# Handing tile 3's normalization to ScalarE and tile 1's to VectorE, and splitting a power on GpSimd, in the prologue of a transformer block

## The chip, the cores and the metric

The kernel runs on one core of a Trainium2 chip. The metric is device time in microseconds of one launch; the lower the better. In the profile the engines are PE (TensorE, matmuls), PEld (its weight loads), DVE (VectorE), ACT (ScalarE), POOL (GpSimd) and SP (SyncE); L1596 is line 1596 of the kernel. The profile also records the clock that TensorE was granted, 1.000 being full speed.

## The reference, cut to what matters

One transformer block over a sequence of 2048 rows of 512 columns: layer norm, a modulation by `1 + ca` and `sa` that come from a small vector `c` through `silu` and a matrix, attention with 32 heads over a window of 512 cached keys, a residual, a second modulated layer norm and a dense layer with relu.

```
def _layernorm(x, axis=-1, eps=1e-05):
    m = jnp.mean(x, axis=axis, keepdims=True)
    v = jnp.var(x, axis=axis, keepdims=True)
    return (x - m) / jnp.sqrt(v + eps)
...
mod = (_silu(c) @ w_mod).reshape(c.shape[0], 6, 1, -1)
...
h = _layernorm(x, axis=-1) * (1 + ca) + sa
x = x + ga * _A_ref(h, A_k_cache, A_v_cache, A_wq, A_wo)
```

The change concerns only the first of these layer norms, and of it only the first block of 512 rows: four tiles of 128 rows x 512 columns. The first projection and the scores of this block wait for them.

## The kernel before: the parts that the change touches

Every instruction goes to one engine's stream, in program order, with the semaphores that its inputs need. `warm(n)` issues n dummy matmuls of 512 columns whose results nobody reads. The statistics of tiles 0, 1, 2 are VectorE's (`ln_stat`), those of tile 3 are ScalarE's (a sum, then a sum of squares into `s3`).

```
    # rstd = (var + eps) ** -0.5, the power on GpSimd, hi - lo columns
    def rstd_pow(lo, hi):
        kb.op(POOL, lambda e: e.tensor_tensor(rstd[:, lo:hi], rstd[:, lo:hi], cst[:, 0:1].to_broadcast([P, hi - lo]), op=ALU.pow), ...)
    ...
    ln_stat(0)
    warm(3, [R_mv[0]])          # dummies, after the statistics of tile 0
    ln_stat(1)
    warm(2, [R_mv[1]])
    rstd_add(0, 2)
    rstd_pow(0, 2)
    kb.op(POOL, ...)            # bias for tile 1: -mean * rstd
    kb.op(ACT, ...)             # ScalarE normalizes tile 1
    silu_mul()
    ln_stat(2)
    rstd_add(2, 3)
    rstd_pow(2, 4)              # tiles 2 and 3 in one instruction
    ln_norm(0)                  # VectorE normalizes tile 0
    kb.op(POOL, ...)            # GpSimd normalizes tile 3
    ...
    fs = mod_cols_mm(0, QBK)    # 32 one-column matmuls on four pieces of w_mod
    for f in fs:
        f()
    ln_tposes(0, TB[0])
    mod_cols_evac(0, QBK)       # VectorE: the modulation vectors, called modc
    ...
    ln_tposes(1, TB[0])
    warm(2, bk=6)
    ln_norm(2)                  # VectorE normalizes tile 2
    mod_half(0, 0, DVE); mod_half(0, 2, ACT)     # modulation of tiles 0 and 1
    ln_tposes(2, TB[1]); ln_tposes(3, TB[1])
    mod_half(0, 1, DVE); mod_half(0, 3, ACT)
    q_half(0, 0, CC_ORDER, QBK)                  # first projection, first half
    mod_half(1, 0, DVE); mod_half(1, 2, ACT); mod_half(1, 1, DVE); mod_half(1, 3, DVE)
    ...                                          # second half, then the scores
```

## Time and profile before

| | us |
|---|---|
| time, median of the first three runs | 560.69 (560.68 to 560.93) |
| span in the profile | 558.9 |
| VectorE's first normalization (tile 0) starts; ScalarE's of tile 1 starts at 7.74 | 7.94 |
| first score matmul starts | 12.41 |

The page and the chain that ended last are read in the prediction below. One more view: TensorE alone in the first 14 us of the kernel before. Columns: start in us, duration in us, engine, line, operation, output and inputs, shapes, count; in brackets the idle time and who ended it.

```profile
8.40 0.62 PE L1377 MATMUL psS<-ident,xn 128*128 128x128 bf16 x8
...
9.42 0.34 PE L1377 MATMUL psS<-ident,xn 128*128 128x128 bf16 x3
...
9.97 0.34 PE L1377 MATMUL psS<-ident,xn 128*128 128x128 bf16 x3 [0.16 <-POOL xn L1613]
...
12.41 0.59 PE L1374 MATMUL psS<-qT,kT 128*128 128x512 bf16 x2 [0.17 <-DVE qT L1620]
```

The transposes of tiles 0 and 1 run together from 8.40, those of tile 2 start at 9.42, those of tile 3 only at 9.97, when GpSimd has finished. The last line is the first score matmul. From there TensorE is busy to the end (98% of the span in the page; 13.89 us of the 14 from 14 to 28 us), so its start is the figure to watch.

### The profile page before, as it was taken

Reading aid. Unit: us, or ns where it says so; the run is one execution under the profiler, and the core shown is the slowest. Engines: PE = TensorE matmul, PEld = TensorE weight load, DVE = VectorE, ACT = ScalarE, POOL = GpSimd, SP = SyncE. Lnnn points to the kernel's source line nnn. Section 1 sums busy time; section 2 is a strip of 40 time slices with the busy share of each in tenths; the row PEclk is TensorE's granted clock in tenths of the full one; section 3 lists DMA queues with packets and bytes.
Section 4 is the critical chain, followed back from the end, with each engine's and each line's share of the span. In section 5 each row is a group of like instructions: output and inputs, shape, how many; then the busy total and the mean of one; then the engine's idle time right before and its main releaser. Section 6 shows DMA issues by size and latency. Waiting matters only on the chain.

```text
span 558.9 us, 9675 instructions
## 1 busy us (share of the span) xinstructions
PE 549.5 (98%) x4061; PEld 315.5 (56%) x4135; DVE 254.7 (46%) x555; ACT 349.3 (63%) x453; POOL 53.3 (10%) x50
## 2 busy tenths in 40 slices
PE   8999999999999999999999999999999999999997
PEld 4665555555555555555555555555555554444444
DVE  4455555553546544335445443333354438322134
ACT  5986666666666666666666666666666644432500
POOL 2000022004410000033000000332000000000000
PEclk9999999999999999999999999999999999999999
DMA  9999662522225144353352412121214110200001
GB/s 258 257 203 192 137 162 47 114 43 73 39 41 74 39 84 106 62 129 58 95 95 56 76 40 39 39 38 38 39 39 76 39 29 0 49 28 22 21 29 48
DMA packets 113357, 42.66 MB, mean 76 GB/s; under 512 B 93977, under 2 KB 112153, under 8 KB 113305
## 3 DMA queue, kind: packets, MB, share of 16 engines
q1 hardware_dynamic: 112584, 41.08, 35.5%
q10 hardware_dynamic: 720, 0.89, 0.5%
q8 instruction: 33, 0.54, 0.4%
q14 instruction: 20, 0.16, 0.1%
HBM read 18.35 MB, written 2.10 MB: 37 GB/s over the span
## 4 chain that ended last, share of the span: by engine, by line
PE 97%; issue 1%; DVE 1%; DMA 1%; POOL 0%
PE psS L1374 28%; PE psO L1374 27%; PE psQ L1374 23%; PE psW L1374 19%; DMA x<-in_A_x_dram 1%; DVE st L1384 0%; POOL xn L1613 0%; POOL rstd L1596 0%; DVE mv L1385 0%; DVE qT L1620 0%; PE psS L1377 0%; DVE rstd L1593 0%; DVE PT L1734 0%; DVE PT L1736 0%; DVE tmp L1424 0%
## 5 line engine op out<-in xcount | busy, mean ns | idle before, releaser
L1498 ACT ACTIVATE PT<-psS 128x1024 bf16<-128x1024 f32 x256 | 262.7, 1028 | 128.7 <-PE psS L1374 128.5
L1374 PE MATMUL psS<-qT,kT 128*128 128x512 bf16 x510 | 151.4, 379 | 0.3 <-DVE qT L1620 0.2
L1374 PEld LDWEIGHTS psO<-v,PT 128*128 128x128 bf16 x2048 | 126.6, 98 | 30.2
L1374 PE MATMUL psO<-v,PT 128*128 128x129 bf16 x2048 | 137.0, 220 | 0.0
L1374 PE MATMUL psQ<-hT,wq 128*128 128x512 bf16 (+1 forms) x509 | 130.2, 377 | 0.2
L1508 DVE RECIPROCAL rinv<-psO 128x4 f32<-128x4 f32 x128 | 23.3, 182 | 225.6 <-PE psO L1374 225.6
L1374 PE MATMUL psW<-wo,oT 128*128 128x512 bf16 x452 | 118.1, 379 | 3.1
L1509 DVE TENSOR_TENSOR o<-psO,rinv 128x512 bf16<-128x512 f32 x128 | 88.5, 691 | 4.5
L1374 PEld LDWEIGHTS psQ<-hT,wq 128*128 128x128 bf16 x512 | 49.9, 98 | 59.8 <-DVE qT L1488 0.4
L1374 PEld LDWEIGHTS psS<-qT,kT 128*128 128x128 bf16 x512 | 49.6, 98 | 58.8 <-ACT PT L1498 0.5
L1490 ACT ACTIVATE qT<-psQ 128x512 bf16<-128x512 f32 x125 | 74.1, 593 | 0.0
L1723 ACT ACTIVATE wq<-psS 128x512 bf16<-128x512 f32 x56 | 33.4, 597 | 49.1 <-PE psS L1374 49.1
L1374 PEld LDWEIGHTS psW<-wo,oT 128*128 128x128 bf16 x512 | 44.9, 98 | 32.9 <-DVE acc L1531 1.2
L1531 DVE TENSOR_TENSOR acc<-psW,acc 128x512 f32<-128x512 f32 x48 | 33.2, 691 | 6.7 <-PE psW L1374 6.7
L1374 PE MATMUL psO<-wmw,wq 128*128 128x512 bf16 (+1 forms) x165 | 32.8, 352 | 0.2
L1534 POOL TENSOR_TENSOR acc<-acc,gaf 128x512 f32<-128x512 f32 x12 | 15.6, 1301 | 146.8 <-DVE acc L1531 139.8
L1390 POOL TENSOR_TENSOR rstd<-rstd,cst 128x4 f32<-128x4 f32 x7 | 7.2, 1025 | 215.7 <-DVE rstd L1389 215.7
L1734 DVE TENSOR_TENSOR PT<-psO,gbf 128x512 f32<-128x512 f32 (+1 forms) x12 | 7.5, 624 | 40.4 <-PE psO L1374 40.4
L1374 PE MATMUL psS<-h2T,wmw 128*128 128x512 bf16 x110 | 25.2, 379 | 0.1
L1374 PEld LDWEIGHTS psO<-wmw,wq 128*128 128x128 bf16 x168 | 15.3, 98 | 16.6
L1374 PE MATMUL psS<-hT,wmw 128*128 128x512 bf16 x110 | 24.4, 379 | 0.1
L1384 DVE BATCH_NORM_STATS2 st<-x 128x6 f32<-128x512 bf16 x31 | 21.1, 680 | 3.6 <-DMA x<-in_A_x_dram 3.6
(90 smaller groups left out, 192.0 us busy)
## 6 DMA issues: line engine op xcount, KB each, us to landing
wo<-in_A_wo_dram SPq DMA_DIRECT2D x4, 1024.0 KB, 6.5
wq<-in_A_wq_dram SPq DMA_DIRECT2D x7, 512.0 KB, 4.6
wmw<-in_B_w_dram SPq DMA_DIRECT2D x14, 256.0 KB, 3.1
wmw<-in_w_mod_dram SPq DMA_DIRECT2D x4, 512.0 KB, 5.1
oT<-o SPq DMA_TRANSPOSE x128, 2.4
out_dram<-PT SPq DMA_DIRECT2D x15, 128.0 KB, 1.7
x<-in_A_x_dram SPq DMA_DIRECT2D x3, 512.0 KB, 4.4
v<-in_A_v_cache_dram SPq DMA_DIRECT2D x8, 128.0 KB, 4.1
```

The costliest lines, as they stand in the source:

```text
L1374: kb.op(PE, lambda e: e.matmul(out_ap, lhsT, rhs, start=start, stop=stop), reads=reads, group_writes=[R_b[k] for k in bk], signal=signal)
L1384: kb.op(DVE, lambda e: e.bn_stats(st[:, t, :], x_sb[:, t, :]), reads=[R_x[t]], writes=[R_st[t]])
L1390: kb.op(POOL, lambda e: e.tensor_tensor(rstd[:, sl], rstd[:, sl], cst[:, 0:1].to_broadcast([P, hi - lo]), op=ALU.pow), reads=R_rstd[sl] + ...
L1490: kb.op(ACT, lambda e: e.activation(qT[u % NQT][:, :], bank[bk], ACTF.Copy), reads=[R_b[bk]], writes=[R_qT[u % NQT]])
L1498: kb.op(ACT, lambda e: e.activation(PT[u % NPT][:, pr * 2:pr * 2 + 2, :], s_ps[pr][:, :, :], ACTF.Exp, scale=scale), reads=[R_b[pr * 2], R ...
L1508: kb.op(DVE, lambda e: e.reciprocal(rinv[:, u, :], o_ps[:, :, P]), reads=[R_b[5], R_b[6]], writes=[R_rinv])
L1509: kb.op(DVE, lambda e: e.tensor_tensor(o_sb[u % NOS][:, :, :], o_ps[:, :, 0:P], rinv[:, u, :].unsqueeze(2).to_broadcast([P, TPB, P]), op=A ...
L1531: kb.op(DVE, lambda e: e.tensor_tensor(acc[:, tl, :], bank[WBK], acc[:, tl, :], op=ALU.add), reads=[R_b[WBK], R_acc[tl]], writes=[R_acc[tl]])
L1534: kb.op(eng, lambda e: e.tensor_tensor(acc[:, tl, :], acc[:, tl, :], gaf[:, :], op=ALU.mult), reads=[R_acc[tl], R_ga], writes=[R_acc[tl]])
L1723: kb.op(ACT, lambda e: e.activation(h1T[b % 2][:, fc, :], bank[bk], ACTF.Relu), reads=[R_b[bk]], writes=[R_h1[b % 2][fc]], pre=all_events( ...
L1734: kb.op(DVE, lambda e: e.tensor_tensor(yt[i][:, c0:c1], bank[bk][:, c0:c1], gbf[:, c0:c1], op=ALU.mult), reads=[R_b[bk], R_gb], writes=[R_ ...
```

## The change

Its intent: let tile 3 not wait for GpSimd's 512-column normalization. ScalarE, which took that tile's statistics, normalizes it; VectorE takes tile 1, which ScalarE had; GpSimd raises tile 3's variance to its power on its own, earlier, and tile 2's afterwards.

```
     rstd_pow(0, 2)
-    kb.op(POOL, lambda e: e.tensor_scalar(s3[:, 3:4], mv[:, 1, 0:1], rstd[:, 1:2], -1.0, op0=ALU.mult, op1=ALU.mult), ...)
-    kb.op(ACT, lambda e: e.activation(xn[:, 1, :], x_sb[:, 1, :], ACTF.Identity, bias=s3[:, 3:4], scale=rstd[:, 1:2]), ...)
+    rstd_pow(3, 4)
+    kb.op(POOL, lambda e: e.tensor_tensor(s3[:, 3:4], s3[:, 1:2], rstd[:, t3:t3 + 1], op=ALU.mult), ...)
+    kb.op(ACT, lambda e: e.activation(xn[:, t3, :], x_sb[:, t3, :], ACTF.Identity, bias=s3[:, 3:4], scale=rstd[:, t3:t3 + 1]), ...)
     silu_mul()
     ln_stat(2)
     rstd_add(2, 3)
-    rstd_pow(2, 4)
+    rstd_pow(2, 3)
     ln_norm(0)
-    kb.op(POOL, lambda e: e.tensor_scalar(xn[:, t3, :], x_sb[:, t3, :], s3[:, 1:2], rstd[:, t3:t3 + 1], op0=ALU.add, op1=ALU.mult), ...)
+    ln_norm(1)
```

(The lists of reads and writes are cut; t3 is 3.)

More of the change, by code (lines that the diff above doesn't have):

```diff
@@ L1604, in build_fast @@
     rstd_pow(0, 2)
-    kb.op(POOL, lambda e: e.tensor_scalar(s3[:, 3:4], mv[:, 1, 0:1], rstd[:, 1:2], -1.0, op0=ALU.mult, op1=ALU.mult), reads=[R_mv[1], R_rstd[1]], writes=[R_nmr])
-    kb.op(ACT, lambda e: e.activation(xn[:, 1, :], x_sb[:, 1, :], ACTF.Identity, bias=s3[:, 3:4], scale=rstd[:, 1:2]),
-          reads=[R_x[1], R_nmr, R_rstd[1]], writes=[R_xn[1]])
+    rstd_pow(3, 4)
+    kb.op(POOL, lambda e: e.tensor_tensor(s3[:, 3:4], s3[:, 1:2], rstd[:, t3:t3 + 1], op=ALU.mult), reads=[R_s3, R_rstd[t3]], writes=[R_nmr])
+    kb.op(ACT, lambda e: e.activation(xn[:, t3, :], x_sb[:, t3, :], ACTF.Identity, bias=s3[:, 3:4], scale=rstd[:, t3:t3 + 1]),
+          reads=[R_x[t3], R_nmr, R_rstd[t3]], writes=[R_xn[t3]])
     silu_mul()
@@ L1610, in build_fast @@
     rstd_add(2, 3)
-    rstd_pow(2, 4)
+    rstd_pow(2, 3)
     ln_norm(0)
-    kb.op(POOL, lambda e: e.tensor_scalar(xn[:, t3, :], x_sb[:, t3, :], s3[:, 1:2], rstd[:, t3:t3 + 1], op0=ALU.add, op1=ALU.mult),
-          reads=[R_x[t3], R_rstd[t3], R_s3], writes=[R_xn[t3]])
+    ln_norm(1)
     TB = [[0, 0, 2, 2], [1, 1, 3, 7]]
```

## The prediction

> **What bounds the kernel now.** I read the page's shares first, then its chain of work that ended last, then the order of instructions in the first 14 us, then the list of who waited for whom there. The page's first two parts:
>
> ```profile
> PE 549.5 (98%) x4061; PEld 315.5 (56%) x4135; DVE 254.7 (46%) x555; ACT 349.3 (63%) x453; POOL 53.3 (10%) x50
> ...
> PE   8999999999999999999999999999999999999997
> ```
>
> TensorE is busy for 98% of the 558.9 us span; only the first slice (14 us) and the last are below 9 tenths. The edited lines run once each, all before 10 us, so all that the change can touch is that first slice: the preparation of block 0 (statistics of four 128x512 tiles of x, normalization, transposes, modulation, first projection). From 14 us on TensorE works without visible gaps, so a shift of the first score matmul should move the end one for one, and nothing larger is to be had. The chain that ended last, windowed to the prologue, in order of time (start us, us, what):
>
> ```profile
> 7.87 0.17 DVE rstd L1593
> 8.04 0.07 issue
> 8.11 0.81 POOL rstd L1596
> 8.92 0.10 issue
> 9.02 0.91 POOL xn L1613
> 9.93 0.05 issue
> 9.97 0.34 PE psS L1377 x3
> 10.31 0.06 PE psW L1377
> 10.37 0.44 PE psQ L1374 x4
> ```
>
> This is what the change attacks. The last of the four tiles (tile 3) is normalized by GpSimd: it waits for VectorE's variance of tile 2, since both powers are one instruction (8.11, 0.81 us), then GpSimd normalizes 512 columns (9.02, 0.91 us), and only then can TensorE transpose it. The statistics of tile 3, taken on ScalarE, were done long before: its rstd input is written at 6.65 + 0.29 = 6.94 us. So tile 3's power waits more than a microsecond for a number that it doesn't need. The instructions around it, each engine asked alone (start us, us, engine, line):
>
> ```profile
> 6.65 0.29 ACT L1590 ACTIVATE rstd<-s,cst 128x1 f32<-128x1 f32 x1
> 7.74 0.81 ACT L1606 ACTIVATE xn<-x,s,rstd 128x512 bf16<-128x512 bf16 x1 [0.80 <-POOL s L1605]
> 9.06 1.02 ACT L1640 ACTIVATE hT<-psS,modc 128x256 bf16<-128x256 bf16 x2 [0.51 <-PE psS L1377]
> ...
> 7.94 0.40 DVE L1395 TENSOR_SCALAR xn<-x,mv,rstd 128x512 bf16<-128x512 bf16 x1
> 8.36 0.17 DVE L1440 TENSOR_TENSOR modc<-psQ,m 128x8 f32<-128x8 f32 x1
> 8.95 0.41 DVE L1395 TENSOR_SCALAR xn<-x,mv,rstd 128x512 bf16<-128x512 bf16 x1 [0.42 <-POOL rstd L1596]
> 9.28 0.72 DVE L1638 TENSOR_SCALAR hT<-psS,modc 128x256 bf16<-128x256 bf16 x2
> 10.41 0.73 DVE L1638 TENSOR_SCALAR hT<-psS,modc 128x256 bf16<-128x256 bf16 x2 [0.41 <-PE psW L1377]
> ```
>
> ScalarE normalizes tile 1 at 7.74 and sits 0.51 us idle after it; VectorE idles 0.42 us before normalizing tile 2 and 0.41 us before the second half of the modulation. These last 0.41 us end with tile 3's transposes and are the prize: VectorE's first modulation pair ends at 10.00, so the second can't start before about that.
>
> [...] the second power, which overlaps the normalization of tile 0, took 804 ns against 717 for the first, so 0.09 us. [...]
>
> **The change part by part.** (1) ScalarE's tile 1 and GpSimd's bias for it go; a second VectorE normalization follows the first. In the blocks that come later two such normalizations take 0.73 us together, so 0.33 us from start to start: tile 1 runs 8.27 to 8.67, against 8.55 before (+0.12). Its transposes end near 9.13 instead of 9.02, and the 128x8 modulation sum slips from 8.36 to about 8.60, which still comes before its first reader.
> (2) The power of tile 3 alone. Four columns took 1.01 us, two 0.72, so an estimate of 0.147 us a column gives 0.57 for one. After the first power (6.62 + 0.72 = 7.34) and the 0.10 us that GpSimd needed between dependent instructions: 7.44 to 8.01.
> (3) The product for ScalarE's bias, one column: 0.26 us, as the one that it replaces: 8.11 to 8.37.
> (4) The power of tile 2, now one column and behind these two: start 8.37 to 8.47, end 8.94 to 9.04. Before, the pair ended at 8.91. Tile 2's normalization so starts at about 9.05 instead of 8.95, ends 9.45, and the modulation behind it starts at 9.38 instead of 9.28.
> (5) ScalarE normalizes tile 3 from 8.41 to 9.22, where GpSimd finished at 9.92: 0.70 us sooner. GpSimd's 0.90 us are gone. But ScalarE's first modulation pair now starts at 9.25 instead of 9.06 and ends at 10.27 instead of 10.08.
> (6) TensorE transposes tile 2 then tile 3 in program order. Tile 2 is there at 9.51; its four transposes start 0.06 us apart, so tile 3 follows at 9.74 without a wait and lands at about 10.14 (0.18 to the last start and 0.22 for itself). Before: 10.15 + 0.22 = 10.37. **Gain 0.23 us.**
> (7) From there: VectorE's second pair at 10.17 (it is free at 10.1), then its last modulation at 10.81 to 11.21 in place of 11.05 to 11.45. The four 256-column matmuls that wait for it, two copies of 0.42 us, and the first score matmul follow unchanged: 12.41 becomes about 12.18. ScalarE's +0.19 doesn't set this: its last first-half output at 10.27 delays one matmul of the first half projection, and the second-half projection waits for VectorE until 11.2 anyway.
>
> The critical release thus changes owner: from tile 3 on GpSimd to tile 2 behind a longer GpSimd queue. Of the 0.70 us won on tile 3 only 0.23 are left, since tile 2 got 0.10 later and VectorE's earlier pair caps the rest.
>
> **The rivals.** R1[...]: two VectorE normalizations now run back to back, 7.94 to 8.67, exactly when GpSimd wants its product and its last power. If each costs 0.09 us, as seen once above, tile 2 comes 0.15 to 0.2 us later and the gain shrinks to 0.05 us or so. [...] Against this: only 0.09 us of delay where 0.23 of overlap were there (8.11 to 8.34). R2, the third power instruction: GpSimd's fixed cost rather than its columns could dominate; with 0.72 for each single-column power instead of 0.57 tile 2 comes 0.3 us later and the gain is zero; the four-column row of 1.01 speaks against it. R3, ScalarE becomes the bound: it holds if the product is late, since tile 3 delays the modulation of the first half on the same engine; it would have to slip by half a microsecond more. R4, hidden anyway: if the first projections wait for a load, an earlier hT brings nothing; the list of waits shows no such wait on a load after 8.2 us, so I put little on it.
>
> **Range and chances.** Half for the plain path (−0.23 us), a third for partial collisions (−0.1 to 0), the rest for a loss of 0.1 to 0.3: −0.23 × 0.5 − 0.05 × 0.33 + 0.2 × 0.17 is about −0.1. From 560.69 that gives 560.6, or 560.5 if I lean on the most likely path; I state 560.5 us. The three runs before spread over 0.25 us (560.68 to 560.93), as large as the effect, and another chip or session may add some tenths, so the range is 559.9 to 561.2. Two per cent is 11.2 us, nearly the whole prologue (12.4 us to the first score matmul): no outcome of these instructions reaches it. Chances: faster 0.005, same 0.99, slower 0.005.
>
> **What would show it right or wrong.** In the changed kernel's first 13 us: a one-column power of 0.55 to 0.6 us starting near 7.4 (step 2); ScalarE's normalization starting near 8.4 (3, 5); tile 2's normalization starting at 9.0 to 9.1 (4), where a start past 9.3 means R1 or R2, told apart by whether the powers are long everywhere or only beside VectorE's normalizations; tile 3's transposes following tile 2's without a wait and ending near 10.14 (6); the first score matmul near 12.2 (7). GpSimd's normalization must be missing from the chain that ended last. The prediction is wrong if the first score matmul moves by some tenths and the end doesn't follow, or if a stage past 14 us differs in length.

The gain of 0.23 us comes from the trace's numbers and the estimates made from them (step 5 takes the 0.81 us of tile 1's normalization), and 560.69 - 0.23 = 560.46, stated as 560.5. The loss of 0.1 to 0.3 us in the weighted sum (-0.1, so 560.6) is the author's estimate, and nothing in the text works out such a loss.

## The result, and the profile after

| | before | after |
|---|---|---|
| median of six runs, us | 560.71 | 560.45 |
| range, us | 560.58 to 561.01 | 560.23 to 562.34 |
| ratio of the runs called fast | | 1.0005 (0.9988 to 1.0021) |

A ratio is the mean time of one kernel's fast runs over that of the other's in the same rounds, so it isn't quite the ratio of the medians. Here the two even point to different sides, and the list of runs shows why: 560.23, 560.36, 560.36, 560.54, and then 562.31 and 562.34. The two long runs count as fast in the ratio, as they lie within 1.5% of the others, but their record shows a mean granted TensorE clock of 0.997, the other four 1.000. So there are two levels, 1.9 us apart, and the change's own effect is a fraction of that. The profile after fell on a run of the upper level. Its page:

```profile
span 560.5 us, 9749 instructions
...
PEclk8999999999999999999999999999999999999999
```

The second line is the granted clock in 40 slices, in tenths; before had 9 in all of them, here the first slice has 8. The profile after asked for busy time and clock in short stretches (columns: stretch in us; length; busy us and count of PE, PEld, DVE, ACT, POOL; granted clock; DMA share; GB/s):

```profile
8.50:9.00 0.50, 0.36 (x13) 0.30 (x11) 0.30 (x1) 0.50 (x1) 0.38 (x1) 1.00 0.63 42
9.00:9.50 0.50, 0.50 (x11) 0.50 (x8) 0.41 (x2) 0.11 (x1) 0.00 (x0) 0.59 0.50 128
9.50:10.00 0.50, 0.50 (x4) 0.25 (x3) 0.23 (x2) 0.16 (x1) 0.00 (x0) 0.50 1.23 232
...
12.50:13.00 0.50, 0.50 (x7) 0.43 (x6) 0.10 (x1) 0.32 (x2) 0.00 (x0) 1.00 1.28 283
```

TensorE works at half clock from about 9.1 us to 12.5 us. (These views count the time before the record's first clock entry as full clock; more on this below.) The run's chain of work that ended last, in the prologue, says a second thing (start us, us, what):

```profile
2.05 6.60 DMA wmw<-in_w_mod_dram
...
8.70 0.35 PE psQ L1374 x8
...
11.51 0.85 PE psQ L1374 x4
```

The modulation weights landed at 8.65 us, so the one-column matmuls on them ended late; from there on the chain is TensorE itself, slow: the four first projection matmuls take 0.85 us where the chain of before had 0.44 (shown in the prediction). Neither the clock nor the load is in any line that the change touches. What it does touch went as planned. GpSimd and ScalarE of the profile after, each asked alone:

```profile
6.76 1.24 POOL L1596 TENSOR_TENSOR rstd<-rstd,cst 128x2 f32<-128x2 f32 x2 [4.64 <-DVE tmp L1423]
8.07 0.19 POOL L1606 TENSOR_TENSOR s<-s,rstd 128x1 f32<-128x1 f32 x1
8.24 0.64 POOL L1596 TENSOR_TENSOR rstd<-rstd,cst 128x1 f32<-128x1 f32 x1
...
8.30 0.81 ACT L1607 ACTIVATE xn<-x,s,rstd 128x512 bf16<-128x512 bf16 x1 [1.21 <-POOL s L1606]
```

The first row holds two powers, of two columns and of one. GpSimd's normalization is gone, and ScalarE has tile 3 ready at 9.11 in place of 9.92.

So two questions are left for the chip: what the change is worth at full clock, and by which of its parts; and whether the half clock belongs to the change.

### The profile page after: what moved, and what is told of

Same layout as the page of the kernel before. It is cut to its first block, busy times and chain, and to the rows that moved or that the text cites. A ratio compares the mean times of both kernels' runs of the same rounds, so it can differ in the third digit from the quotient of the medians.

```text
span 560.5 us, 9749 instructions
## 1 busy us (share of the span) xinstructions
PE 555.3 (99%) x4135; PEld 316.8 (57%) x4135; DVE 255.0 (45%) x556; ACT 349.4 (62%) x453; POOL 52.8 (9%) x50
## 4 chain that ended last, share of the span: by engine, by line
PE 98%; DMA 1%; SPq 0%; DVE 0%; issue 0%
PE psS L1374 28%; PE psO L1374 27%; PE psQ L1374 23%; PE psW L1374 20%; DMA wmw<-in_w_mod_dram 1%; PE psS L1377 0%; SPq L1303 0%; DVE qT L1620 0%; DVE PT L1734 0%; DVE PT L1736 0%; PE psW L1377 0%
## 5 line engine op out<-in xcount | busy, mean ns | idle before, releaser
L1374 PE MATMUL psW<-wo,oT 128*128 128x512 bf16 x512 | 130.6, 379 | 0.0
```

Of the source, the lines that this page charges most:

```text
L1374: kb.op(PE, lambda e: e.matmul(out_ap, lhsT, rhs, start=start, stop=stop), reads=reads, group_writes=[R_b[k] for k in bk], signal=signal)
```

## The experiments

All kernels of one set ran on one chip beside before, and all gave correct results. In what follows a run counts as **full clock** if its record shows 0.999 or 1.000, and as **low clock** at 0.997 or less; the sets below compare full-clock runs with full-clock runs, by their means. The start of the first score matmul is counted from VectorE's first instruction of `silu_mul` (L1423), since the arrival of x shifts everything (this instruction starts between 6.25 and 6.59 us in the fourteen profiles); it is 12.41 - 6.44 = 5.97 us in the kernel before. "Wait for w_mod" is VectorE's idle time before the `modc` sum, when it waits for the one-column matmuls.

| run | edit | low clock | full-clock mean, us (before, same set) | L1423 to first scores, us | wait for w_mod, us |
|---|---|---|---|---|---|
| again | the change | 1 of 6 | 560.32 (560.74) | 5.59 | none |
| again_2 | the change | 1 of 6 | 560.39 (560.78) | 5.60 | none |
| again_3 | the change | 1 of 5 | 560.51 (560.75) | 6.16 | 0.58 |
| split_only | power split alone | 2 of 6 | 560.52 (560.74) | 5.95 | 0.64 |
| split_only_2 | the same | 1 of 5 | 560.70 (560.75) | 6.07 | 0.82 |
| joint_power | new assignment alone | 0 of 5 | 561.05 (560.74) | 6.31 | none |
| act_product | product on ScalarE | 0 of 5 | 560.48 (560.74) | 5.60 | none |
| no_filler | without 2 late dummies | 0 of 5 | 560.27 (560.64) | 5.56 | none |
| more_filler | 3 more dummies | 0 of 5 | 560.43 (560.64) | 5.62 | none |
| moved_filler | both | 0 of 5 | 560.55 (560.64) | 6.04 | 0.51 |
| late_weights | w_mod requested later | 1 of 5 | 560.97 (560.64) | 6.18 | 0.61 |
| no_gated_dummies | without 5 early dummies | 4 of 5 | see text | 7.55 (low) | 0.47 |

The last two columns are from the one profiled run of each.

### The change itself, again

No edit.

> The changed kernel itself, once more. Theory M (as predicted): with TensorE at full clock the first score matmul starts 0.2 to 0.3 us earlier than the 12.41 us of before, and the end follows: fast-clock runs 0.2 to 0.4 us below before (about 560.3 to 560.5). Theory C: the runs at 562.3 are those in which the record shows a mean clock of 0.997, that is TensorE at half clock for some 3.3 us of the first 14; they cost 1.7 to 2.0 us, and are either peculiar to the change (C1: before never shows them) or a matter of when the run starts (C2: before shows some too, when it is run as often). Rival N: two levels without connection to the clock.

Measured: 559.99 to 560.89 us in five full-clock runs and 562.01 in one low one. The mean of the five is 0.42 us below that of before. **Before showed the low clock as well**: 562.88 and 562.25 us, both at 0.997, in 2 of its 11 runs. So C1 falls: the upper level isn't peculiar to the change. N falls too, since every long run of this set has the low record. Theory M is right, and the gain is larger than it said. The chain that ended last, in the prologue, of this full-clock run of the change:

```profile
8.00 0.33 DVE xn L1395
...
8.38 0.72 PE psS L1377 x8
9.10 0.43 PE psO L1374 x2
9.53 0.17 PE psS L1377 x3
```

GpSimd is out of the chain altogether. The transposes of tile 2 (9.53) follow two dummies (`psO`, 0.43 us), which is what `no_filler` below asks about. VectorE and TensorE of the same run, each asked alone:

```profile
8.76 0.41 DVE L1395 TENSOR_SCALAR xn<-x,mv,rstd 128x512 bf16<-128x512 bf16 x1
...
10.02 0.73 DVE L1638 TENSOR_SCALAR hT<-psS,modc 128x256 bf16<-128x256 bf16 x2 [0.15 <-PE psW L1377]
...
9.59 0.33 PE L1377 MATMUL psS<-ident,xn 128*128 128x128 bf16 x3
...
12.01 0.59 PE L1374 MATMUL psS<-qT,kT 128*128 128x512 bf16 x2 [0.17 <-DVE qT L1620]
```

Tile 2's normalization starts at 8.76 where before had 8.95. The two lines ahead of it, of VectorE and of GpSimd, each asked alone, say why:

```profile
7.84 0.15 DVE L1593 TENSOR_SCALAR rstd<-mv 128x1 f32<-128x1 f32 x1
...
8.08 0.64 POOL L1596 TENSOR_TENSOR rstd<-rstd,cst 128x1 f32<-128x1 f32 x1
```

The power of tile 2 starts 0.08 us after the end of its input (7.84 + 0.15 = 7.99), as it did in before (7.87 + 0.15 = 8.02, then 8.11): GpSimd's longer queue doesn't hold it up. It is shorter, 0.64 us for one column where the pair of columns took 0.80.

Tile 3's transposes start at 9.59 where before had 9.97, VectorE's second modulation pair at 10.02 where before had 10.41, and the first scores at 12.01 where before had 12.41.

### Only the power split

```
     rstd_pow(0, 2)
     ...                       # tile 1 stays on ScalarE
+    rstd_pow(3, 4)
     silu_mul()
     ...
-    rstd_pow(2, 4)
+    rstd_pow(2, 3)
     ln_norm(0)
     ...                       # tile 3 stays on GpSimd
```

> Only the power is split; tile 1 stays on ScalarE, tile 3 on GpSimd. Theory M: tile 3 still comes last and behind the power of tile 2 on the same engine; the GpSimd queue gets one instruction longer, so tile 3 is ready at 9.9 to 10.0 as before: first score matmul 12.4 to 12.5, time within 0.1 us of before. Rival S (the split itself is the gain): 0.2 us faster than before.

Measured: full-clock mean 0.22 us below before, by four runs. That is what rival S had said, not theory M. But the first scores came only 0.02 us earlier (5.95 against 5.97), because this profiled run had late weights. GpSimd and VectorE of it, each asked alone:

```profile
8.72 0.77 POOL L1614 TENSOR_SCALAR xn<-x,s,rstd 128x512 bf16<-128x512 bf16 x1
...
9.03 0.60 DVE L1395 TENSOR_SCALAR xn<-x,mv,rstd 128x512 bf16<-128x512 bf16 x1
```

Two readings. GpSimd finishes tile 3 at 9.49, where it took until 9.92 before; theory M had said 9.9 to 10.0 and was wrong, since the powers of one column are shorter (start to start 0.53 and 0.55 us) and the first of them runs before the variance of tile 2 is there. And the two normalizations get into each other's way: here GpSimd started first and VectorE's took 0.60 us instead of 0.41; in the kernel before VectorE started first (8.95), and GpSimd's took 0.90 instead of 0.77. So each took longer where it was the second to start, GpSimd's by 0.13 us and VectorE's by 0.19. In split_only_2, where VectorE's came only in the last 0.27 us of GpSimd's, it took 0.42 us, so there was next to no price.

Since the profile didn't fit the times, the split was run again, with the change beside it:

> The split power alone once more, because its first profile fell into a run with late modulation weights (VectorE waited 0.64 us for them) and its times at full clock lay 0.22 us under before, not within 0.1 as theory M had said. Theory S (the split is most of the gain: GpSimd's powers and its normalization now end at 9.5 instead of 9.9): with the weights on time tile 2's normalization starts by 8.8, the first score matmul at 12.0 to 12.1, full-clock mean 0.3 to 0.4 us under before, as the whole change. Theory M2 (split and assignment each give a part): first score matmul 12.15 to 12.3, full-clock mean 0.1 to 0.25 us under before.

> The whole change beside it on the same chip. Full-clock mean 0.4 us under before (0.40, 0.42 and 0.39 in the three sets so far), first score matmul at 11.9 to 12.1. Theory S: no more than 0.1 us faster than the split alone; theory M2: 0.15 to 0.3 us faster.

Measured: the split 0.05 us below before by four full-clock runs, the change 0.24. Both profiled runs had late weights again, and so neither says where the first scores would start with the weights on time. VectorE of the change in this run, and TensorE ahead of it:

```profile
9.40 0.17 DVE L1440 TENSOR_TENSOR modc<-psQ,m 128x8 f32<-128x8 f32 x1 [0.58 <-PE psQ L1374]
...
9.01 0.35 PE L1374 MATMUL psQ<-sc_bf,wmw 128*128 128x1 bf16 x8 [0.19 <-DMA wmw<-in_w_mod_dram]
```

VectorE has tiles 0 and 1 done and waits 0.58 us for the last weights; `ln_norm(2)` stands behind `modc` in its stream, so tile 2 waits too, whatever GpSimd does. In the runs with such a wait the first scores follow the start of the `modc` sum by nearly the same time: 12.75 - 9.40 = 3.35 us here, 12.66 - 9.31 = 3.35 in split_only_2, 3.40 in split_only, 3.34 in late_weights. **With late weights the change and the split alone are equal to 0.05 us**, and what the change earns on GpSimd is hidden by the wait. How before does with late weights isn't shown: its one profile had them on time.

Over all sets the full-clock means are 560.39 us for the change (18 runs), 560.61 for the split alone (8) and 560.73 for before (43): the change is 0.34 us faster (plus or minus 0.15, a 95% interval from the spread of the runs), the split 0.12 (plus or minus 0.18). The numbers lean to M2, in which each part gives something; but the split's part isn't clear of noise, and S and M2 aren't told apart for sure. The record's interval leaves out 1 only for no_gated_dummies (1.0030, 1.0017 to 1.0043).

### Only the new assignment

```
-    rstd_pow(3, 4)
...                            # product and ScalarE's normalization moved down
-    rstd_pow(2, 3)
+    rstd_pow(2, 4)
+    kb.op(POOL, ...)          # product
+    kb.op(ACT, ...)           # ScalarE normalizes tile 3
```

> Only the assignment is changed: ScalarE normalizes tile 3 and VectorE tile 1, but the power of tiles 2 and 3 stays one instruction behind the variance of tile 2. Theory M: the power ends near 8.9, the product near 9.2, ScalarE's normalization runs 9.3 to 10.1, and ScalarE's modulation of the first half is pushed behind it: first score matmul 12.6 to 12.7, 0.2 to 0.3 us slower than before. Rival S2 (taking GpSimd off the 512 columns is the gain): 0.1 to 0.2 us faster than before.

Measured: 0.31 us slower than before, first scores 0.34 us later, all as theory M said. ScalarE and TensorE of it:

```profile
9.20 0.81 ACT L1610 ACTIVATE xn<-x,s,rstd 128x512 bf16<-128x512 bf16 x1 [2.23 <-POOL s L1609]
...
10.06 0.34 PE L1377 MATMUL psS<-ident,xn 128*128 128x128 bf16 x3 [0.27 <-ACT xn L1610]
```

ScalarE sits idle for 2.23 us, then normalizes until 10.01, and its share of the modulation comes after. **Without the split the reassignment is a loss**: tile 3 comes no earlier than from GpSimd (10.06 against 9.97), and ScalarE is taken away from its next work. The change lives on the early power: in one set, the same assignment with the power split (again) is 0.73 us faster than without (plus or minus 0.34).

### The product on ScalarE, and the dummies between the transposes

Two tries to gain more at full clock. In the first the one-column product moves:

```
-    kb.op(POOL, lambda e: e.tensor_tensor(s3[:, 3:4], s3[:, 1:2], rstd[:, t3:t3 + 1], op=ALU.mult), ...)
+    kb.op(ACT, lambda e: e.activation(s3[:, 3:4], s3[:, 1:2], ACTF.Copy, scale=rstd[:, t3:t3 + 1]), ...)
```

> As the change, but the one-column product runs on ScalarE instead of GpSimd, so that the power of tile 2 need not stand behind it. Theory M (tile 2 behind the longer GpSimd queue now sets the end of the transposes): power of tile 2 from about 8.1 to 8.7, tile 2 normalized from about 8.8, transposes of tile 3 end about 0.2 us earlier than in the change; 0.1 to 0.2 us faster than the change. Rival V (VectorE's first modulation pair or ScalarE's is the cap): no gain over the change.

Measured: 5.60 us to the first scores, the same as the change (5.59), and 0.26 us below before. Rival V was right: no gain. Tile 2's power can't start before its variance is there: it starts at 8.19 in this run, 0.08 us after its input, which is what the change has with the product in the way. So theory M's queue wasn't the limit.

In the second the two dummies between the transposes go (`- warm(2, bk=6)`):

> As the change, without the two 512-column dummy matmuls that TensorE runs between the transposes of tiles 1 and 2. Theory F (with the change tile 2 is ready at 9.17 us but its transposes start only at 9.37, since TensorE is still in the dummies): transposes of tile 2 start within 0.1 us of the end of its normalization, first score matmul 0.1 to 0.15 us earlier than in the change, full-clock runs 0.1 us faster than the change. Theory C (the 562 us runs come from too little TensorE activity in one interval of some 3.4 us): more runs at a mean clock of 0.997 than the 3 of 12 of the change. Rival V: VectorE's first modulation pair caps it, no gain at full clock.

Measured: 5.56 us to the first scores, so 0.03 us better than the change, and 0.37 us below before, as the change. Theory F's 0.10 to 0.15 didn't come. The chain that ended last of this run now does pass GpSimd:

```profile
6.58 1.25 POOL rstd L1596 x2
...
7.90 0.19 POOL s L1606
8.09 0.62 POOL rstd L1596
...
8.74 0.42 DVE xn L1395
```

Tile 2's release by GpSimd is thus close to the limit now, as the prediction had it, but not because of the queue: the chain is led over the product, which ends just ahead of this power, while the power again starts 0.08 us after its input (7.83 + 0.15 = 7.98, then 8.06 in GpSimd's own view). Right behind it VectorE runs four modulations without a gap (9.12, 1.48 us). The limits lie within some hundredths of a microsecond of each other, so taking one away wins almost nothing. And theory C's forecast for this run, more runs at low clock, failed as well: 0 of 5.

### Where the half clock comes from

Cutting the stretches of the profile after finer (0.93 granted in 9.0 to 9.1 us, 0.75 in 12.4 to 12.6) gives half clock from 9.09 to 12.50, so for 3.41 us, at 0.50. Neighbouring transposes start about 0.105 us apart there and 0.055 at full clock (three in 0.52 us of which the last takes 0.31, and three in 0.33 of which the last takes 0.22). What halves the clock this profile doesn't show. Theory C holds too little TensorE work responsible; that its interval is some 3.4 us long, as this stretch is, is an assumption. Four experiments asked.

More dummies among the one-column matmuls, and the same without the two later ones:

```
     fs = mod_cols_mm(0, QBK)
-    for f in fs:
+    for i, f in enumerate(fs):
+        if i in (8, 16, 24):
+            warm(1)
         f()
```

> As the change, with three more 512-column dummy matmuls, one ahead of the second, third and fourth group of eight one-column matmuls that wait for the pieces of the modulation weights. Theory C: TensorE is active through the wait for these pieces, so no run at 0.997. Its price: up to 0.2 us at full clock, if the dummies delay the transposes of tiles 0 and 1. Rival C3 (the clock drops for reasons outside of TensorE's work): 0.997 in about a fifth to a quarter of the runs as in the others.

> Both: the two dummies after tile 1's transposes removed, the three among the groups of one-column matmuls added. Theories C and F: no run at 0.997, and at full clock as fast as no_filler, 0 to 0.15 us faster than the change. If C is wrong, 0.997 in a quarter of the runs.

Measured: no low-clock run in 5 and in 5, which fits theory C but says little, since no_filler, joint_power and act_product had none either. Their price in the first scores is 0.03 us for more_filler; in moved_filler the first scores come 0.45 us later than in the change, with `modc` at 8.99. That isn't the price of the dummies alone: in this run TensorE got its full clock only at 6.99 us (below), and the five dummies ahead took 1.92 us, where again had 1.37 (no_filler, with full clock at 6.51, had 1.69).

The weights requested after the first projection's weights instead of ahead of them:

```
-    for i in range(DC):
-        load_wm01(i, (ACT, SP)[i % 2])
     for i, eng in enumerate((SP, SP)):
         dma(wq_sb[:, 2 * i:2 * i + 2, 0:QA * Dh], ...)
+    for i in range(DC):
+        load_wm01(i, (ACT, SP)[i % 2])
```

> As the change, but the four pieces of modulation weights are requested after the first projection's weights, so that they land some 0.5 to 0.7 us later. Theory C with the late pieces as the trigger: TensorE idles longer between the groups of one-column matmuls, and most runs show 0.997 and lie near 562 to 562.5 us. Rival: late pieces only shift the prologue, by up to 0.6 us at full clock, with 0.997 as often as before.

Measured: one low-clock run in 5, and at full clock 0.33 us slower than before. The rival was right: late weights shift the prologue (0.59 us against the change), and don't bring the low clock by themselves.

The last one takes away the five dummies that TensorE runs after the statistics of tiles 0 and 1 (`- warm(3, [R_mv[0]])`, `- warm(2, [R_mv[1]])`); beside it the change ran once more. (The expectation of again_2 counts 7 of 35 runs; with the nine runs of before in the second set it should have read 44.)

> As the change, without the five 512-column dummy matmuls that TensorE runs between 5.6 and 7.0 us, so that from 5.6 to 8.4 us it has only 32 one-column matmuls. Theory C (clock lost through too little TensorE work in one interval): nearly all runs at 0.997 or below, the record showing half clock for some 3.3 us ending near 12 to 13 us, at 562 to 562.5 us. Rival C3 (the low clock comes from outside): 0.997 in about one of six runs, the rest at 560.1 to 560.5 us.

> The changed kernel a third time, to narrow the size at full clock and the frequency of the lower one. Theory M: mean of the full-clock runs 0.3 to 0.5 us below that of before (the first score matmul was 0.38 us earlier, counted from the same VectorE instruction). Theory C2: 0.997 in some runs of either kernel, about one in six of all so far (7 of 35 runs of before, the change and the split power).

Measured: again_2 is 0.39 us below before at full clock, with one low run of 6, and before has one of 11. Without the five dummies all five runs lie between 562.11 and 563.23 us; four of them are recorded at 0.997 or 0.993, and one, of 562.68, at 1.000. Busy time and clock of it, in stretches of one microsecond:

```profile
8.00:9.00 1.00, 0.88 (x26) 0.80 (x27) 0.60 (x2) 0.81 (x1) 0.68 (x2) 0.93 0.88 72
9.00:10.00 1.00, 0.90 (x9) 0.85 (x8) 0.55 (x3) 0.06 (x1) 0.00 (x0) 0.50 0.90 189
...
12.00:13.00 1.00, 1.00 (x10) 0.83 (x8) 0.69 (x3) 0.69 (x3) 0.00 (x0) 0.86 1.19 305
```

The same picture as in the profile after: half clock from 8.9 to 12.3 us, and 562 us. So **theory C is shown in its main point: what holds the clock in the prologue is the work that TensorE is given around 5.6 to 7 us**, and too little of it cost 2.2 us (the five runs average 562.56 us, the change beside them 560.39 at full clock; the weights, late in the profile, may be a part of that). With the five dummies in place the clock is lost only now and then: in 3 of 46 runs of before, 5 of 23 of the change, 3 of 11 of the split, 1 of the other 30 kernels' runs that keep them. (The six runs of before in the first set lie at 561.01 us or less and are counted as full, though not each has its clock on record.)

What decides it in a single run is open. The clock's changes don't fall at one place in every run. Each kept trace has a list of them, which the views above only average: its first entry, the grant of full clock, lies anywhere from 3.79 us (again_3) to 6.99 us (moved_filler), at 3.92 in before, 5.57 in again and 5.67 in the profile after. The halving came 3.41 us after that in both profiles that have it, and the return 3.41 us after the halving, within 0.01: 5.67, 9.09 and 12.50 us in the profile after, 5.45, 8.86 and 12.28 in no_gated_dummies. That the place of the first entry decides isn't shown: again had nearly the same one and kept its clock. Nor does TensorE's busy time ahead of the halving decide by itself. Between the first entry and the halving it had 2.7 us of 3.41 in the profile after and 1.3 in no_gated_dummies, yet late_weights kept its clock through a stretch of the same length (7.22 to 10.63 us) with 2.5, as far as the matmuls are on record.

Whether the change makes the loss more frequent (5 of 23 against 3 of 46) can't be settled by so few runs either. And the run of 562.68 us recorded at full clock is unexplained. A first entry that came very late would look like this, since the time before it counts as full clock (moved_filler, with its first entry at 6.99 us, is recorded at 1.000); that run left no trace to tell.

How much of the 1.9 us is clock? In the profile after the first scores come 7.39 us after L1423, with the weights late as well. late_weights, whose weights were later still, took 6.18 at full clock. So at least 1.2 us are the clock's. From the start of the `modc` sum, by which the weights are there in both, it is 4.88 us (13.97 - 9.09) against 3.34, so about 1.5.

## Why the prediction was right or wrong

- **The end result**: 560.5 was forecast, with 559.9 to 561.2; the median is 560.45. The direction at full clock and the class were right. That the median came so close is partly luck: it mixes four runs near 560.4 with two near 562.3, and the two lie outside the range.
- **Only the prologue counts, and its shift reaches the end one for one**: right. The first scores came 0.38 us earlier (5.97 to 5.59), the full-clock times 0.42 and 0.39 us in the two sets whose profile had the weights on time.
- **Step 2, a one-column power of 0.57 us**: right, 0.554. Its start was mis-sized: I gave it the 0.10 us that dependent GpSimd instructions had taken in before. It depends on nothing in the queue, and started 0.03 us before the previous power ended. R2, a fixed cost of 0.72 us for any power, falls with the 0.554.
- **Step 3, the product of 0.26 us**: 0.19, and ScalarE's normalization started at 8.14 (again) and 8.30 (after) in place of 8.41. R3, ScalarE as the bound, didn't come: in again its first modulation started at 9.13 and had waited 0.18 us for TensorE.
- **Step 4, tile 2 later by 0.10 us**: this is the step that failed, and with it the sentence that the release passes to "tile 2 behind a longer GpSimd queue". With the two errors above summed, the queue was out of the way in time; tile 2's power started 0.08 us after its own input, as before, took 0.64 us in place of 0.80 and ended at 8.72. Its normalization started at 8.76, so 0.19 us **earlier** than before. I had it 0.10 later, hence a gain of 0.23 in step 6 instead of 0.38.
- **Step 6, the transposes of tile 3 follow those of tile 2 without a wait**: right (9.37 and 9.59). I hadn't seen that TensorE would be held by its own dummies until 9.37; no_filler shows that it costs 0.03 us at most.
- **Step 7, 12.18 for the first scores**: 12.01, by the 0.15 us of step 4.
- **R1, GpSimd beside VectorE's normalizations**: there, but of the size seen before (0.64 us for the power beside them against 0.55 for the one ahead of them), no more.
- **R4, a load**: I put little on it, since the one trace of before showed no wait on a load after 8.2 us. That was a step too far from a single run: in five of the twelve later profiles with the usual order of loads (after, both of the split, again_3, no_gated_dummies) the weights came late, and then they set the first scores and hide what the change earns on GpSimd.
- **Not foreseen**: the low clock. The range was drawn from three runs of before, none of which had it.

Over all runs, low ones included, the change averages 560.79 us (23 runs) and before 560.84 (46): the gain at full clock is real and 0.06% of the time, and the two levels of the clock are five times as far apart.

## What to carry to other kernels

When several small results share an engine, compute each as soon as its own input is there: splitting one instruction in two can pay although the two take longer together (powers of 0.55 and 0.64 us here, where the one for both columns took 0.80). Here it was worth 0.73 us with the new assignment, which lost 0.3 us without it; alone, its gain isn't clear of noise. A prologue in which three engines and a load all finish within some tenths of a microsecond has no single bottleneck; take away one limit and the next stands right behind, so look at all of them before expecting a sum. And before reading a difference of a few tenths, list the single runs with their clock: a mean or a median can be a mixture of two levels.

## What the traces showed of the hardware

- A power on GpSimd took 0.554 us for one column, 0.72 for two, 1.01 for four, by the profile's spans, on 128 partitions in fp32; 0.64 to 0.65 for one column with VectorE's normalizations beside it.
- On GpSimd an independent instruction started 0.03 us before the end of the last one; a dependent one started 0.08 to 0.10 us after the end of the one that it needed.
- Where a GpSimd instruction and a VectorE normalization overlapped, the one that started second took 0.09 us more (a power) or 0.13 to 0.19 us more (a normalization that overlapped the other engine's for 0.34 to 0.46 us), and 0.01 us more for an overlap of 0.27. So the price was less than the overlap of the two spans each time. The profile doesn't tell in which part of its span an instruction is held up.
- How much TensorE work keeps the clock isn't shown: five dummies of 512 columns, 32 one-column matmuls and a few transposes were enough in most runs and not in some (12 of the 110 runs with the five dummies were low), and without the five dummies all five runs were at the slow level. The half clock lasted 3.41 us in the profile after and as long, within 0.01, in no_gated_dummies.
- The clock's records fit the matmuls: in the profile after, ten dummies of 512 columns took 4.45 us ahead of the first entry (full clock at 5.67 us), and the five after it 1.40 us. But the views of the profile show 1.00 from the start, since they count the time before the first entry as full clock. Full clock in the view is no proof of it in the first microseconds.
